# A linear-attention block and a SoLU feed-forward block on one core: a fixed, software-pipelined order on TensorE, with attention five chunks ahead of the input product and that three ahead of the output product

## The chip, the core and the metric

The kernel runs on one core of one Trainium2 chip. The core has five engines, each with its own instruction queue taken in order: TensorE (PE in the profile, with its weight loads listed as PEld), VectorE (DVE), ScalarE (ACT), GpSimd (POOL) and SyncE (SP), which here only starts DMA transfers. Matrix products are written to a small memory called PSUM, and DVE or ACT copy them out. The metric is the device time of one execution in microseconds (us). The profiler lists the clock that was granted to TensorE, as a share of full speed; in this kernel it is 1.0 or 0.5, and shares between these are means.

## The reference

Two blocks follow each other. The first is a recurrence over 768 steps for 4 batches and 8 heads of width 48; the second takes its 3072 x 384 output through two matrix products with a softmax-weighted activation and a normalisation between them.

```python
for t in range(S):
    cur = np.einsum('bhd,bhe->bhde', u[None] * kt, vt)
    y[:, :, t] = np.einsum('bhd,bhde->bhe', rt, state + cur)
    state = w[None, :, :, None] * state + np.einsum('bhd,bhe->bhde', kt, vt)
...
h = x @ w_in                                  # 3072 x 384 times 384 x 1024
sm = softmax(h)
solu = h * sm
ln = (solu - mean(solu)) / np.sqrt(var(solu) + 1e-06) * g_ln
out = ln @ w_out                              # 3072 x 1024 times 1024 x 384
```

## The kernel before

The sequence is cut into 6 chunks of 128 steps. A unit is one batch and one chunk, so there are 24 units; they go chunk by chunk with the four batches side by side, so the state that a unit needs was made four units earlier. A unit is also 128 rows of the feed-forward block.

In a unit, `prepare` (line 590) weighs k with powers of w on POOL (tile `kp`), multiplies r, u and k for the diagonal (`rku`, `own`), writes the diagonal into the score tile `AT`, and turns r and the weighed k on PE (`tr_ps`, `tk_ps`, copied to `rT` by DVE and to `kT` by ACT). `scores` (618) makes the 128 x 128 scores of each head (`at`) and DVE copies their upper triangle into `AT`. `finish` (631) makes the output of attention (`y_ps`, from the state and from `AT` and v), copies it to `x`, and updates the state (`kv_ps`). `ffn_in` (661) turns x (`xt_ps`, copied to `xT`), makes the input product `h_ps`, and lets DVE, ACT and POOL do softmax, product and normalisation, in this order: maximum, exponential, division, `solu`, squares, power, normalised `solu`. `ffn_out` (693) turns `solu` (`t_ps`, copied to `lnT` by halves, the first by DVE and the second by ACT), makes the output product `o_ps`, copies it to `o` and stores it.

The weights come as 64-bit floats, in 14 pieces. `load_weights` fetches a piece as pairs of 32-bit words (`raw`), and `convert` makes 32-bit floats of it with seven operations on DVE and one or two on POOL.

The loop at the end (713 to 736) sets the order in which the code names the work: a load two units ahead, `prepare` one ahead, up to five conversions, `ffn_in` of the unit three back (`LAG`), `scores`, `ffn_out` of the unit three back, `finish`. A scheduler then orders each engine's queue from this, by the code's order and its own estimate of when each operation can start; so on PE the matmuls of different functions may change places. PSUM holds four tiles for everything called `m` (`tr_ps`, `tk_ps`, `y_ps`, `kv_ps`, `xt_ps`, `t_ps`, `o_ps`), two for the scores, and one `h_ps`.

`direct_path` holds all of this; `general_path`, for values of w outside 0.75 to 1.25, stands behind a branch that these inputs do not take.

Of the kernel before, what the change touches and what calls it, by code (L numbers as in the profile page):

```python
# [9 lines left out]
F32 = mybir.dt.float32  # L10
U32 = mybir.dt.uint32
# [385 lines left out]
def direct_path(  # L397
# [56 lines left out]
    def load(i):  # L454
        b, c = units[i]
        for t, src in ((kpads, k), (rpads, r), (vts, v)):
            nc.sync.dma_start(out=t[i % NLD][:, :, 0:D],
                              in_=src[b, :, ts(c, T), :].rearrange("h s d -> s h d"))
# [9 lines left out]
    for q in range(2):  # L468
# [19 lines left out]
    raws = {}  # L488

    def load_weights(j):  # L490
        dst, src, _ = pieces[j]
        raws[j] = wpool.tile([128, dst.shape[1], 2], U32, tag="raw", name="raw", bufs=6)
        nc.scalar.dma_start(out=raws[j].rearrange("p n o -> p (n o)"), in_=src)
# [30 lines left out]

    for j in range(6):
        load_weights(j)
# [14 lines left out]
    for j in range(7):  # L541
        n = 1 << j
# [41 lines left out]
    live = {}  # L584

    def pair(t, a):
        return t[:, 2 * a : 2 * a + 2, :].rearrange("p q d -> p (q d)")


    def prepare(i):  # L590
        b, c = units[i]
        kt, rt = kpads[i % NLD], rpads[i % NLD]
        X = live[i] = {}
        X["kp"] = kp = apool.tile([128, H, P], F32, name="kp")
        nc.gpsimd.tensor_mul(kp.rearrange("p h d -> p (h d)"),  # L595
                             kt.rearrange("p h d -> p (h d)"),
                             kdec.rearrange("p a d -> p (a d)"))
        rku = apool.tile([128, H, D], F32, name="rku")
        nc.gpsimd.tensor_mul(rku, kt[:, :, 0:D], u_bc)  # L599
        nc.gpsimd.tensor_mul(rku, rku, rt[:, :, 0:D])  # L600
        own = small.tile([128, H, 1], F32, name="own")
        nc.vector.tensor_reduce(out=own[:, :, 0], in_=rku, axis=AX.X, op=ALU.add)  # L602
        AT = X["AT"] = apool.tile([128, H, T], F32, name="AT")
        nc.gpsimd.tensor_mul(AT, ident.unsqueeze(1).to_broadcast([128, H, T]),  # L604
                             own.to_broadcast([128, H, T]))
        X["kT"] = apool.tile([128, HP, T], F32, name="kT")
        X["rT"] = apool.tile([128, HP, T], F32, name="rT")
        ps = psM.tile([128, HP, T], F32, tag="m", name="tr_ps")
        for a in range(HP):
            nc.tensor.transpose(ps[:, a, :], pair(rt, a), ident)  # L610
        nc.vector.tensor_mul(X["rT"], ps, fore)
        ps = psM.tile([128, HP, T], F32, tag="m", name="tk_ps")
        for a in range(HP):
            nc.tensor.transpose(ps[:, a, :], pair(kp, a), ident)  # L614
        nc.scalar.copy(out=X["kT"], in_=ps)  # L615
# [15 lines left out]
    def finish(i):  # L631
        b, c = units[i]
        X = live[i]
        vt, AT, St = vts[i % NLD], X["AT"], states[b]
        y_ps = psM.tile([128, H, D], F32, tag="m", name="y_ps")
# [7 lines left out]
        for h in range(H):  # L643
            nc.tensor.matmul(y_ps[:, h, :], AT[:, h, :], vt[:, h, :],  # L644
                             start=first, stop=(h == H - 1), skip_group_check=True)
            first = False
        x = X["x"] = fpool.tile([128, dm], F32, name="x", bufs=LAG + 1)
        nc.scalar.copy(out=x, in_=y_ps.rearrange("p h d -> p (h d)"))
# [11 lines left out]

    def ffn_in(i):
        X = live[i]
        xt_ps = psM.tile([128, KD, 128], F32, tag="m", name="xt_ps")
        for j in range(KD):
            nc.tensor.transpose(xt_ps[:, j, :], X["x"][:, ts(j, 128)], ident)
        xT = fpool.tile([128, KD, 128], F32, name="xT")
        nc.scalar.copy(out=xT, in_=xt_ps)  # L667
        h_ps = psH.tile([128, dff], F32, name="h_ps")
        for n in range(dff // NX):
            for j in range(KD):  # L670
                nc.tensor.matmul(h_ps[:, ts(n, NX)], xT[:, j, :], w_in_sb[:, j, ts(n, NX)],  # L671
                                 start=(j == 0), stop=(j == KD - 1))
# [6 lines left out]
        nc.vector.reciprocal(out=rs, in_=rs)  # L679
        solu = X["solu"] = fpool.tile([128, dff], F32, name="solu")  # L680
        nc.vector.scalar_tensor_tensor(out=solu, in0=h_ps, scalar=rs, in1=e,  # L681
# [10 lines left out]

    def ffn_out(i):
        b, c = units[i]
        X = live.pop(i)
        lnT = fpool.tile([128, KF, 128], F32, name="lnT")
        for g in range(KF // 4):
            t_ps = psM.tile([128, 4, 128], F32, tag="m", name="t_ps")
            for f in range(4):
                nc.tensor.transpose(t_ps[:, f, :], X["solu"][:, ts(4 * g + f, 128)], ident)  # L700
            if g % 2 == 0:
                nc.vector.tensor_copy(out=lnT[:, ts(g, 4), :], in_=t_ps)
            else:
                nc.scalar.copy(out=lnT[:, ts(g, 4), :], in_=t_ps)
        o_ps = psM.tile([128, dm], F32, tag="m", name="o_ps")
        for f in range(KF):
            nc.tensor.matmul(o_ps, lnT[:, f, :], w_out_sb[:, f, :],  # L707
                             start=(f == 0), stop=(f == KF - 1))
        o = fpool.tile([128, dm], F32, name="o")
        nc.scalar.copy(out=o, in_=o_ps)  # L710
        nc.sync.dma_start(out=out[ds(b * S + c * T, T), :], in_=o)

    N = len(units)
    todo = list(range(len(pieces)))
    ahead = 6
    prepare(0)
    for i in range(N + LAG):
        j = i - LAG
        if i + 2 < N:
            load(i + 2)  # L720
        if i + 1 < N:
            prepare(i + 1)
        for _ in range(5):
            if todo:
                convert(todo.pop(0))
                if ahead < len(pieces):
                    load_weights(ahead)
                    ahead += 1
# [51 lines left out]
```

## Time and profile before

| | |
|---|---|
| time, median of 3 runs | 825.41 us (824.98 to 825.49) |
| the profiled execution's own time | 824.45 us |
| its span, first to last instruction | 822.7 us |
| mean granted TensorE clock | 0.768 |
| matmuls on PE | 2220 |
| DMA | 25.83 MB, mean 31 GB/s |

The span is what the profiler's rows cover; the time has some 1.75 us more around it. A busy share is an average over a start (until about 100 us, in which the weights are converted), a steady part, and an end. The rows in the next parts give for each group or instruction its start, its duration, the line of the code, the tiles (output<-inputs) and, in brackets, how long the engine stood idle before it and what released it.

### The profile page before, as it was taken

The numbers are of one execution on the slowest core, as the hardware profiler recorded it, in microseconds if no ns is written. First come the engines' busy times: TensorE is split into PE (matmuls) and PEld (weight loads), VectorE is DVE, ScalarE is ACT, GpSimd is POOL, SyncE is SP. The second block draws the span as 40 slices with busy tenths as digits, with TensorE's granted clock in tenths as the row PEclk, the third lists the DMA queues.
The fourth block names the chain that finished last, engine by engine and source line by source line (L and its number), as shares of the span: only waits on it lengthen the run. The fifth ranks groups of instructions, "written<-read, shape, count | busy, mean of one in ns | idle before, by whom it ended". The sixth has DMA issues, their size and how long they took to land.

```text
span 822.7 us, 5801 instructions
## 1 busy us (share of the span) xinstructions
PE 548.8 (67%) x2220; PEld 351.4 (43%) x2220; DVE 249.9 (30%) x441; ACT 121.2 (15%) x217; POOL 184.3 (22%) x193
## 2 busy tenths in 40 slices
PE   0344575867768568658677686596686696656764
PEld 0244443634535435435345354354353464334332
DVE  6999633122131230231321312212212312221121
ACT  0100011111110110111111101111111212121111
POOL 4655702202212112032022121220220201000000
PEclk9955587778768867877787687777777887789886
DMA  9632101101101011011011010110100000000000
GB/s 237 133 94 63 29 6 33 39 0 39 37 2 39 20 19 39 10 29 39 1 38 27 13 38 11 29 39 0 39 20 0 19 10 10 0 10 10 10 10 14
DMA packets 81990, 25.83 MB, mean 31 GB/s; under 512 B 76961, under 2 KB 80162, under 8 KB 81954
## 3 DMA queue, kind: packets, MB, share of 16 engines
q1 hardware_dynamic: 78336, 18.88, 11.2%
q10 hardware_dynamic: 3618, 6.50, 2.7%
q8 instruction: 19, 0.31, 0.2%
q14 instruction: 17, 0.14, 0.1%
HBM read 20.65 MB, written 4.72 MB: 31 GB/s over the span
## 4 chain that ended last, share of the span: by engine, by line
PE 60%; DVE 18%; POOL 8%; ACT 8%; issue 4%; DMA 1%; ACTq 0%; POOLq 0%
PE h_ps L671 20%; PE o_ps L707 20%; PE y_ps L644 6%; PE t_ps L700 6%; DVE solu L681 4%; POOL AT L604 4%; ACT sq L685 4%; DVE st L675 4%; ACT e L677 4%; POOL kp L595 3%; DVE solu L689 2%; PE tk_ps L614 2%; PE y_ps L639 2%; PE at L625 2%; POOL st L688 2%
## 5 line engine op out<-in xcount | busy, mean ns | idle before, releaser
L671 PE MATMUL h_ps<-w_in_sb,xT 128*128 128x512 f32 x288 | 169.1, 749 | 2.5 <-ACT xT L667 2.5
L707 PE MATMUL o_ps<-w_out_sb,lnT 128*128 128x384 f32 x384 | 165.1, 594 | 0.0
L700 PE MATMUL t_ps<-ident,solu 128*128 128x128 f32 x192 | 46.6, 424 | 164.8 <-DVE solu L689 164.8
L707 PEld LDWEIGHTS o_ps<-w_out_sb,lnT 128*128 128x128 f32 x384 | 88.8, 239 | 69.4 <-issue 30.5
L700 PEld LDWEIGHTS t_ps<-ident,solu 128*128 128x128 f32 x192 | 37.6, 223 | 171.2 <-issue 166.8
L671 PEld LDWEIGHTS h_ps<-w_in_sb,xT 128*128 128x128 f32 x288 | 67.8, 244 | 89.0 <-issue 83.4
L604 POOL TENSOR_TENSOR AT<-ident,own 128x1024 f32<-128x1024 f32 x24 | 45.7, 1903 | 238.9 <-PE y_ps L644 236.6
L675 DVE TENSOR_REDUCE st<-h_ps 128x1 f32<-128x1024 f32 x24 | 29.4, 1225 | 153.0 <-PE h_ps L671 153.0
L644 PE MATMUL y_ps<-vt,AT 128*128 128x48 f32 x384 | 51.3, 289 | 36.1 <-DVE AT L628 24.9
L686 POOL TENSOR_SCALAR st<-st 128x1 f32<-128x1 f32 x24 | 4.6, 192 | 305.6 <-ACT sq L685 305.6
L644 PEld LDWEIGHTS y_ps<-vt,AT 128*128 128x128 f32 x384 | 50.1, 209 | 37.1 <-DVE AT L628 25.4
L655 DVE TENSOR_TENSOR state<-kv_ps,state 128x384 f32<-128x384 f32 x16 | 8.9, 557 | 167.6 <-PE kv_ps L652 167.6
L677 ACT ACTIVATE e<-h_ps,st 128x1024 f32<-128x1024 f32 x24 | 26.7, 1114 | 207.6 <-DVE st L675 207.6
L614 PE MATMUL tk_ps<-ident,kp 128*128 128x128 f32 x96 | 21.4, 363 | 39.8 <-POOL kp L595 39.8
L625 PE MATMUL at<-rT,kT 48*128 48x128 f32 x384 | 42.3, 347 | 5.4 <-ACT kT L615 3.8
L602 DVE TENSOR_REDUCE own<-rku 128x8 f32<-128x384 f32 x24 | 13.2, 549 | 105.7 <-POOL rku L600 105.7
L625 PEld LDWEIGHTS at<-rT,kT 48*128 48x128 f32 x384 | 31.6, 227 | 28.3 <-issue 16.8
L689 DVE TENSOR_SCALAR solu<-solu,st 128x1024 f32<-128x1024 f32 x24 | 19.5, 812 | 54.1 <-POOL st L688 54.1
L599 POOL TENSOR_TENSOR rku<-kpad,u_bc 128x384 f32<-128x384 f32 x24 | 24.4, 1016 | 46.5 <-DMA kpad<-in_k_dram 46.5
L685 ACT ACTIVATE sq<-solu,st 128x1024 f32<-128x1024 f32 x24 | 27.5, 1147 | 48.3 <-DVE st L683 48.3
L710 ACT COPY o<-o_ps 128x384 f32<-128x384 f32 x24 | 11.5, 479 | 149.3 <-PE o_ps L707 149.3
L614 PEld LDWEIGHTS tk_ps<-ident,kp 128*128 128x128 f32 x96 | 14.5, 184 | 44.3 <-POOL kp L595 44.3
(67 smaller groups left out, 515.9 us busy)
## 6 DMA issues: line engine op xcount, KB each, us to landing
kpad<-in_k_dram SPq DMA_DIRECT2D x24, 192.0 KB, 3.2
rpad<-in_r_dram SPq DMA_DIRECT2D x24, 192.0 KB, 3.8
vt<-in_v_dram SPq DMA_DIRECT2D x24, 192.0 KB, 2.7
out_dram<-o SPq DMA_DIRECT2D x24, 192.0 KB, 1.9
raw<-in_moe_w_in_dram ACTq DMA_DIRECT2D x6, 512.0 KB, 6.6
raw<-in_moe_w_out_dram ACTq DMA_DIRECT2D x8, 384.0 KB, 3.1
u_bc<-in_u_dram ACTq DMA_DIRECT2D x1, 192.0 KB, 3.9
wd<-in_w_dram ACTq DMA_DIRECT2D x2, 0.8 KB, 6.1
```

What stands on the lines that cost most here:

```text
L604: nc.gpsimd.tensor_mul(AT, ident.unsqueeze(1).to_broadcast([128, H, T]), own.to_broadcast([128, H, T]))
L614: nc.tensor.transpose(ps[:, a, :], pair(kp, a), ident)
L625: nc.tensor.matmul(pss[q][:, a, :], X["kT"][rows, a, :], X["rT"][rows, a, :], start=True, stop=True)
L644: nc.tensor.matmul(y_ps[:, h, :], AT[:, h, :], vt[:, h, :], start=first, stop=(h == H - 1), skip_group_check=True)
L671: nc.tensor.matmul(h_ps[:, ts(n, NX)], xT[:, j, :], w_in_sb[:, j, ts(n, NX)], start=(j == 0), stop=(j == KD - 1))
L675: nc.vector.tensor_reduce(out=nmax, in_=h_ps, axis=AX.X, op=ALU.max, negate=True)
L677: nc.scalar.activation(out=e, in_=h_ps, func=ACT.Exp, bias=nmax, accum_out=se)
L681: nc.vector.scalar_tensor_tensor(out=solu, in0=h_ps, scalar=rs, in1=e, op0=ALU.mult, op1=ALU.mult, accum_out=tot)
L685: nc.scalar.activation(out=sq, in_=solu, func=ACT.Square, bias=nmu, accum_out=ss)
L689: nc.vector.tensor_scalar(out=solu, in0=solu, scalar1=nmu, scalar2=rstd, op0=ALU.add, op1=ALU.mult)
L700: nc.tensor.transpose(t_ps[:, f, :], X["solu"][:, ts(4 * g + f, 128)], ident)
L707: nc.tensor.matmul(o_ps, lnT[:, f, :], w_out_sb[:, f, :], start=(f == 0), stop=(f == KF - 1))
```

## The change

All 24 units, all tiles and all operations stay. What changes is their order and the number of buffers.

- `prepare` is split into `weigh` (POOL and DVE work) and `turn` (transposes); the transposes of x leave `ffn_in` as `turn_x`, and those of the normalised values leave `ffn_out` as `turn_ln`.
- The loop runs from -2 to N + 8. In iteration i stand: load of i+4, `weigh` of i+3, `turn` of i+2, two conversions, `ffn_in` of i-5, `turn_ln` of i-8, `scores` of i+1, `ffn_out` of i-8, `finish` of i, `turn_x` of i-4.
- The loop stands under a manual schedule for PE: its queue has exactly the order of the code. The queues of the other engines are ordered by the scheduler as before.
- More buffers: v has 6 tiles for 4, `kp` and `AT` 4 for 2, `rT` 3 for 2, `x` 6 for 4, `solu` 5 for 2. `raw` has 5 for 6.

```diff
-    LAG = 3
+    LA, LO = 5, 3
...
-    NLD = 4
+    NLD, NV = 4, 6
...
-    vts = [const.tile([128, H, D], F32, name=f"vt{i}") for i in range(NLD)]
+    vts = [const.tile([128, H, D], F32, name=f"vt{i}") for i in range(NV)]
...
     load(1)
+    load(2)
+    load(3)
...
-    def prepare(i):
+    def weigh(i):
...
-        X["kp"] = kp = apool.tile([128, H, P], F32, name="kp")
+        X["kp"] = kp = apool.tile([128, H, P], F32, name="kp", bufs=4)
...
-        AT = X["AT"] = apool.tile([128, H, T], F32, name="AT")
+        AT = X["AT"] = apool.tile([128, H, T], F32, name="AT", bufs=4)
...
+    def turn(i):
+        X, rt = live[i], rpads[i % NLD]
         X["kT"] = apool.tile([128, HP, T], F32, name="kT")
-        X["rT"] = apool.tile([128, HP, T], F32, name="rT")
+        X["rT"] = apool.tile([128, HP, T], F32, name="rT", bufs=3)
...
-    def ffn_in(i):
+    def turn_x(i):
         X = live[i]
         xt_ps = psM.tile([128, KD, 128], F32, tag="m", name="xt_ps")
...
+    def ffn_in(i):
+        X = live[i]
         h_ps = psH.tile([128, dff], F32, name="h_ps")
...
-        solu = X["solu"] = fpool.tile([128, dff], F32, name="solu")
+        solu = X["solu"] = fpool.tile([128, dff], F32, name="solu", bufs=LO + 2)
...
-    def ffn_out(i):
-        b, c = units[i]
-        X = live.pop(i)
-        lnT = fpool.tile([128, KF, 128], F32, name="lnT")
+    def turn_ln(i):
+        X = live[i]
+        lnT = X["lnT"] = fpool.tile([128, KF, 128], F32, name="lnT")
...
+    def ffn_out(i):
+        b, c = units[i]
+        X = live.pop(i)
         o_ps = psM.tile([128, dm], F32, tag="m", name="o_ps")
...
-    ahead = 6
-    prepare(0)
-    for i in range(N + LAG):
-        j = i - LAG
-        if i + 2 < N:
-            load(i + 2)
-        if i + 1 < N:
-            prepare(i + 1)
-        for _ in range(5):
-            if todo:
-                convert(todo.pop(0))
...
-        if j >= 0:
-            ffn_in(j)
-        if i < N:
-            scores(i)
-        if j >= 0:
-            ffn_out(j)
-        if i < N:
-            finish(i)
+    ahead = 5
+    weigh(0)
+    weigh(1)
+    with tc.manual_schedule(engines={mybir.EngineType.PE}):
+        for i in range(-2, N + LA + LO):
+            j, l = i - LA, i - LA - LO
+            if 0 <= i and i + 4 < N:
+                load(i + 4)
+            if 0 <= i + 3 and i + 3 < N and i + 3 >= 2:
+                weigh(i + 3)
+            if 0 <= i + 2 < N:
+                turn(i + 2)
+            for _ in range(2):
+                if i >= -1 and todo:
+                    convert(todo.pop(0))
...
+            if 0 <= j < N:
+                ffn_in(j)
+            if 0 <= l < N:
+                turn_ln(l)
+            if 0 <= i + 1 < N:
+                scores(i + 1)
+            if 0 <= l < N:
+                ffn_out(l)
+            if 0 <= i < N:
+                finish(i)
+            if 0 <= j + 1 < N:
+                turn_x(j + 1)
```

**PE, one iteration of the steady part.** PE's queue before, from one input product to the next; the number behind a tile's name tells the copies of it apart, and `solu_1715` is what the softmax makes of `h_ps_1702`. The scores' further rows, which repeat `at0` and `at1`, are left out.

```order
L671 MATMUL h_ps_1702<-w_in_sb_105,xT_1700 128x512 x6
L625 MATMUL at0_1835<-rT_1683,kT_1682 128x128
L625 MATMUL at1_1836<-rT_1683,kT_1682 128x128
L700 MATMUL t_ps_1736<-ident_132,solu_1715 128x128 x4
L700 MATMUL t_ps_1742<-ident_132,solu_1715 128x128 x4
L707 MATMUL o_ps_1748<-w_out_sb_106,lnT_1735 128x384 x8
L639 MATMUL y_ps_1760<-state1_186,rT_1571 128x96 x4
L644 MATMUL y_ps_1760<-vt1_91,AT_1568 128x48 x8
L652 MATMUL kv_ps_1775<-vt1_91,kp_1561 128x96 x4
L610 MATMUL tr_ps_1796<-ident_132,rpad3_85 128x128 x4
L614 MATMUL tk_ps_1802<-ident_132,kp_1785 128x128 x4
L665 MATMUL xt_ps_1808<-ident_132,x_1549 128x128 x3
```

The same stretch of PE's queue now. `solu_1142` belongs to the input product three iterations earlier; that of `h_ps_1465` is `solu_1478`.

```order
L678 MATMUL h_ps_1465<-w_in_sb_107,xT_1437 128x512 x6
L706 MATMUL t_ps_1487<-ident_138,solu_1142 128x128 x4
L706 MATMUL t_ps_1493<-ident_138,solu_1142 128x128 x4
L629 MATMUL at0_1499<-rT_1340,kT_1339 128x128
L629 MATMUL at1_1500<-rT_1340,kT_1339 128x128
L717 MATMUL o_ps_1511<-w_out_sb_108,lnT_1486 128x384 x8
L643 MATMUL y_ps_1523<-state0_191,rT_1228 128x96 x4
L648 MATMUL y_ps_1523<-vt0_90,AT_1113 128x48 x8
L656 MATMUL kv_ps_1538<-vt0_90,kp_1106 128x96 x4
L669 MATMUL xt_ps_1545<-ident_138,x_1088 128x128 x3
L614 MATMUL tr_ps_1565<-ident_138,rpad3_85 128x128 x4
L618 MATMUL tk_ps_1571<-ident_138,kp_1442 128x128 x4
```

The turning of the normalised values now reads a tile of an earlier iteration, the scores stand between it and the output product, and the transposes of x stand ahead of those of r and k.

**DVE, one iteration of the steady part.** DVE's queue before, from the maximum over one `h_ps` on:

```order
L675 TENSOR_REDUCE st_1373<-h_ps_1366 128x1
L628 COPY_PREDICATED AT_1344<-later_167,at0_1499 128x4x128
L628 COPY_PREDICATED AT_1344<-later_167,at1_1500 128x4x128
L678 TENSOR_SCALAR st_1373<-st_1373 128x1
L679 RECIPROCAL st_1373<-st_1373 128x1
L681 SCALAR_TENSOR_TENSOR solu_1379,st_1373<-h_ps_1366,st_1373,e_1375 128x1024
L683 TENSOR_SCALAR st_1373<-st_1373 128x1
L689 TENSOR_SCALAR solu_1379<-solu_1379,st_1373 128x1024
L702 COPY lnT_1399<-t_ps_1400 128x512
L655 TENSOR_TENSOR state2_187<-kv_ps_1439,state2_187 128x384
L611 TENSOR_TENSOR rT_1459<-tr_ps_1460,fore_140 128x512
L602 TENSOR_REDUCE own_1902<-rku_1899 128x8
```

And now:

```order
L682 TENSOR_REDUCE st_1360<-h_ps_1353 128x1
L708 COPY lnT_1374<-t_ps_1375 128x512
L632 COPY_PREDICATED AT_1113<-later_173,at0_1387 128x4x128
L685 TENSOR_SCALAR st_1360<-st_1360 128x1
L632 COPY_PREDICATED AT_1113<-later_173,at1_1388 128x4x128
L686 RECIPROCAL st_1360<-st_1360 128x1
L688 SCALAR_TENSOR_TENSOR solu_1366,st_1360<-h_ps_1353,st_1360,e_1362 128x1024
L690 TENSOR_SCALAR st_1360<-st_1360 128x1
L696 TENSOR_SCALAR solu_1366<-solu_1366,st_1360 128x1024
L659 TENSOR_TENSOR state3_194<-kv_ps_1426,state3_194 128x384
L615 TENSOR_TENSOR rT_1452<-tr_ps_1453,fore_146 128x512
L603 TENSOR_REDUCE own_1783<-rku_1780 128x8
```

The copy of the first half of `lnT` has moved from behind the normalisation to right behind the maximum; the rest of the order is nearly the same. In the start of the program, DVE's queue had up to five conversions between the score copies of two units and now has two.

More of the change, by code (lines that the diff above doesn't have):

```diff
@@ L491, in load_weights @@
         dst, src, _ = pieces[j]
[L492 removed]
+        raws[j] = wpool.tile([128, dst.shape[1], 2], U32, tag="raw", name="raw", bufs=5)
         nc.scalar.dma_start(out=raws[j].rearrange("p n o -> p (n o)"), in_=src)
@@ L523, in convert @@
                                     op0=ALU.mult, op1=ALU.mult)
-    for j in range(6):
+    for j in range(5):
         load_weights(j)
@@ L613, in prepare @@
         for a in range(HP):
-            nc.tensor.transpose(ps[:, a, :], pair(kp, a), ident)
+            nc.tensor.transpose(ps[:, a, :], pair(X["kp"], a), ident)
         nc.scalar.copy(out=X["kT"], in_=ps)
@@ L665, in ffn_in @@
             nc.tensor.transpose(xt_ps[:, j, :], X["x"][:, ts(j, 128)], ident)
-        xT = fpool.tile([128, KD, 128], F32, name="xT")
-        nc.scalar.copy(out=xT, in_=xt_ps)
+        X["xT"] = fpool.tile([128, KD, 128], F32, name="xT")
+        nc.scalar.copy(out=X["xT"], in_=xt_ps)
+    def ffn_in(i):
+        X = live[i]
         h_ps = psH.tile([128, dff], F32, name="h_ps")
@@ L670, in ffn_in @@
             for j in range(KD):
-                nc.tensor.matmul(h_ps[:, ts(n, NX)], xT[:, j, :], w_in_sb[:, j, ts(n, NX)],
+                nc.tensor.matmul(h_ps[:, ts(n, NX)], X["xT"][:, j, :], w_in_sb[:, j, ts(n, NX)],
                                  start=(j == 0), stop=(j == KD - 1))
@@ L704, in ffn_out @@
                 nc.scalar.copy(out=lnT[:, ts(g, 4), :], in_=t_ps)
+    def ffn_out(i):
+        b, c = units[i]
+        X = live.pop(i)
         o_ps = psM.tile([128, dm], F32, tag="m", name="o_ps")
         for f in range(KF):
-            nc.tensor.matmul(o_ps, lnT[:, f, :], w_out_sb[:, f, :],
+            nc.tensor.matmul(o_ps, X["lnT"][:, f, :], w_out_sb[:, f, :],
                              start=(f == 0), stop=(f == KF - 1))
```

13 lines of the change are left out of this document (6 added, 7 removed).

## The prediction

> **What bounds the kernel now.** I read the page's head and its chain of waits first, then the waits of TensorE (PE), then one unit of the steady part on PE's timeline, then the granted clock in windows. The page's first two rows say who works and who ends last (busy us by engine; the chain followed back from the end, as shares of the span):
>
> ```profile
> PE 548.8 (67%) x2220; PEld 351.4 (43%) x2220; DVE 249.9 (30%) x441; ACT 121.2 (15%) x217; POOL 184.3 (22%) x193
> PE 60%; DVE 18%; POOL 8%; ACT 8%; issue 4%; DMA 1%; ACTq 0%; POOLq 0%
> ```
>
> PE is busy for 67% and no engine is full; the chain changes from PE to the others and back. PE's rows of one unit (start, duration; a product of the program stands as two matmuls in the trace, a transpose as one, so h_ps counts 12 for 6):
>
> ```profile
> 403.86 1.94 PE L700 MATMUL t_ps<-ident,solu 128*128 128x128 f32 x8 [6.84 <-DVE solu L689]
> 405.73 6.21 PE L707 MATMUL o_ps<-w_out_sb,lnT 128*128 128x384 f32 x16
> 411.77 1.03 PE L639 MATMUL y_ps<-state,rT 128*128 128x96 f32 x8
> 412.64 1.91 PE L644 MATMUL y_ps<-vt,AT 128*128 128x48 f32 x16
> 414.38 1.10 PE L652 MATMUL kv_ps<-vt,kp 128*128 128x96 f32 x8
> 415.32 0.60 PE L610 MATMUL tr_ps<-ident,rpad 128*128 128x128 f32 x4
> 417.80 1.12 PE L614 MATMUL tk_ps<-ident,kp 128*128 128x128 f32 x4 [1.88 <-POOL kp L595]
> ...
> 420.32 7.43 PE L671 MATMUL h_ps<-w_in_sb,xT 128*128 128x512 f32 x12
> 427.68 0.94 PE L625 MATMUL at<-rT,kT 48*128 48x128 f32 x12
> 435.45 1.94 PE L700 MATMUL t_ps<-ident,solu 128*128 128x128 f32 x8 [6.83 <-DVE solu L689]
> ```
>
> A unit takes 435.45 - 403.86 = 31.6 us. PE stands still for 6.83 us of it, while the softmax and normalisation of the unit whose input product it has just made run on DVE, ACT and POOL, and for 1.88 us until POOL has weighed k. Over the kernel the first wait alone is
>
> ```profile
> PE t_ps L700 <- DVE solu L689: 164.8, 24, 7.7
> ```
>
> 164.8 us in 24 units. The waits cost a second time, through the clock. In windows of 3.41 us (length, PE busy with its count, granted clock, then DMA):
>
> ```profile
> 93.32:96.73 3.41, 3.41 (x18) 0.50 0.15 28
> 96.73:100.14 3.41, 3.41 (x19) 0.50 0.75 144
> ...
> 414.17:417.58 3.41, 1.75 (x16) 1.00 0.29 54
> 417.58:420.99 3.41, 3.15 (x12) 0.50 0.63 118
> ...
> 666.75:670.16 3.41, 3.41 (x32) 1.00 0.16 58
> 670.16:673.58 3.42, 3.07 (x16) 1.00 0.00 0
> ...
> 721.36:724.78 3.42, 2.82 (x27) 1.00 0.16 58
> 724.78:728.19 3.41, 3.41 (x8) 1.00 0.00 0
> ```
>
> The clock changes at the edges of such windows. After a window with 1.75 us of work it falls to half (414.17); after 2.82 us of light matmuls (721.36) and after a window full of them (666.75) it stays full; a full window of light matmuls at half clock does not raise it (93.32). So each long wait is followed by matmuls at half speed: the sixteen of o_ps above take 411.77 - 405.73 = 6.04 us, and at full clock, by the rows below, 5.16.
>
> **The change part by part.** The order on PE is now that of the code: input product of unit i-5, turning of the normalised unit i-8, scores of i+1, output product of i-8, end of attention of i. The normalised values that are turned were finished three units ago, so the 6.83 us wait goes; kp is made two units ahead of its turning, so the 1.88 us go. No matmul is added or removed. What PE then needs for a unit, at full clock:
>
> ```profile
> 149.83 2.74 PE L707 MATMUL o_ps<-w_out_sb,lnT 128*128 128x384 f32 x8
> 152.41 1.03 PE L639 MATMUL y_ps<-state,rT 128*128 128x96 f32 x8
> ...
> 669.90 0.60 PE L614 MATMUL tk_ps<-ident,kp 128*128 128x128 f32 x4
> 670.34 0.49 PE L665 MATMUL xt_ps<-ident,x 128*128 128x128 f32 x3
> ...
> 671.60 5.42 PE L671 MATMUL h_ps<-w_in_sb,xT 128*128 128x512 f32 x12
> 676.94 0.94 PE L625 MATMUL at<-rT,kT 48*128 48x128 f32 x12
> ...
> 724.73 5.42 PE L671 MATMUL h_ps<-w_in_sb,xT 128*128 128x512 f32 x12 [0.60 <-ACT xT L667]
> ```
>
> From start to start: h_ps 676.94 - 671.60 = 5.34; o_ps 2 x 2.58 = 5.16; four transposes 0.44, so tr, tk 0.44 each, t_ps (8) 0.88, xt_ps (3) 0.33; scores 16 x 0.94/12 = 1.25; from the first unit's rows, whose clock was full by then, y_ps 0.87 + 1.74 and kv_ps 0.94. Sum 17.4 us against 31.6. 0.1 us for small waits is an estimate: **17.5 us a unit**.
>
> What hides the rest: the output product needs the first half of lnT, and DVE takes h_ps's maximum before it copies that half:
>
> ```profile
> L675 DVE TENSOR_REDUCE st<-h_ps 128x1 f32<-128x1024 f32 x24 | 29.4, 1225 | 153.0 <-PE h_ps L671 153.0
> L702 DVE COPY lnT<-t_ps 128x512 f32<-128x512 f32 x24 | 16.6, 692 | 30.4 <-PE t_ps L700 30.4
> L677 ACT ACTIVATE e<-h_ps,st 128x1024 f32<-128x1024 f32 x24 | 26.7, 1114 | 207.6 <-DVE st L675 207.6
> L681 DVE SCALAR_TENSOR_TENSOR solu<-h_ps,st,e 128x1024 f32<-128x1024 f32 x24 | 30.8, 1284 | 0.8
> ```
>
> 1.23 + 0.69 and two starts of 0.1 give 2.1 us after h_ps; t_ps and scores cover 0.88 + 1.25 = 2.13. It just fits; where scores are missing, at the end, 1.2 us of wait appear. h_ps has one buffer and comes free after maximum, exponential and product, with DVE's copies between them some 5 us (an estimate from these rows), inside the 12 us until the next h_ps. xT's copy waits beside eight transposes (0.88 us against the 0.60 of the last row); without them, at the end, 0.6 us appear. The output of a unit leaves three units later, which costs nothing but the drain. The deeper buffers (kp, AT, solu, vt) only separate users. One raw buffer fewer delays a weight load until the fifth conversion before it is read; at two conversions an iteration that is hidden.
>
> The start changes most in its order. Five conversions stood ahead of each pair of score copies on DVE, now two. In the old start (last steps of four successive conversions at 78.94 and 89.94, the third unit's last copy, the first input product, and DVE's two larger operations of a unit):
>
> ```profile
> 78.94 1.35 DVE L510 SCALAR_TENSOR_TENSOR ex<-raw,ex 128x384 uint32<-128x384 uint32 x1
> ...
> 89.94 0.55 DVE L510 SCALAR_TENSOR_TENSOR ex<-raw,ex 128x384 uint32<-128x384 uint32 x1
> ...
> 91.96 0.72 DVE L628 COPY_PREDICATED AT<-later,at 128x512 f32<-128x512 uint32 x1
> ...
> 99.96 5.49 PE L671 MATMUL h_ps<-w_in_sb,xT 128*128 128x512 f32 x12
> ...
> L628 DVE COPY_PREDICATED AT<-later,at 128x512 f32<-128x512 uint32 x48 | 32.1, 714 | 0.0
> L611 DVE TENSOR_TENSOR rT<-tr_ps,fore 128x512 f32<-128x512 f32 x24 | 16.3, 681 | 21.2 <-PE tr_ps L610 21.2
> ```
>
> A conversion takes 11.0 / 3 = 3.7 us; a unit of attention 2 x 0.71 + 0.68 and two short ones, which I take at 3.2 in all. The old 92.7 held 14 conversions and three units. The first input product now needs ten conversions and five units: 92.7 - 14.7 + 6.4 = 84, and some 9.5 us of PE at half clock behind it (at, y, kv, xt, tr, tk): 94. All 14 conversions and six units are done at 92.7 + 9.6 = 102; the first softmax comes only then, so the second input product starts near 106, the third 11.6 later (5.34 and 6 of attention), the fourth at **129**. From there both products run in each iteration:
>
> - 12 iterations of 17.5 (units 8 to 19 in attention): 210
> - two without kv (16.56): 33
> - two more without tr and tk, with xT's 0.6: 32.6
> - four without attention, 5.34 + 2.1 + 5.16 + 0.33 + 0.6: 54, and a fifth without xt: 12.6
> - three of t_ps and o_ps alone, 0.88 + 0.6 + 5.16: 19.8
>
> That is 362: the last output product ends at 491. Behind it stands what stands now:
>
> ```profile
> 817.35 0.48 ACT L710 COPY o<-o_ps 128x384 f32<-128x384 f32 x1 [6.36 <-PE o_ps L707]
> ```
>
> 822.7 - 817.35 = 5.4. Span 496.5; the profiled execution took 824.45 us with a span of 822.7, so 498; the median, 825.41, lies 1 above it: **499 us**. The start is the loosest term, 129 within 10 either way; a unit may cost 17.0 (weight loads better hidden) or 18.5 (a microsecond of small waits). That is 482 to 525.
>
> [...] Between two products stand y, kv, xt, tr, tk: 4.8 us of light matmuls, eleven instructions of them transposes. The rows that come nearest: the window at 666.75 has y, tr and tk and stays at full clock, and four tk take 0.44 there, against the eight t_ps at half clock in 1.87 us (403.86 to 405.73), 0.94 for four. So transposes run at full clock and do not lower it here. [...]
>
> **The rivals.**
>
> [...] 10%.
>
> *DVE or POOL behind PE.* An engine that takes its queue in order may stand behind a load: POOL's next unit waits for kpad, whose buffer POOL itself frees.
>
> ```profile
> kpad<-in_k_dram SPq DMA_DIRECT2D x24, 192.0 KB, 3.2
> ```
>
> Round that loop go one landing of 3.2 us and at most POOL's whole work of a unit, 184.3/24 = 7.7: 10.9 us, under 17.5. It decides from a landing of 9.8 us; at 12.3 the unit takes 20, +2.5 over 16 units: 540. POOL then also holds back DVE's `own`, which stands ahead of the next maximum. 6%.
>
> *Slower than before: the clock halves in a dense stream.* The quoted stretch at full clock is two windows long, 6.8 us (666.75 to 673.58); whether hundreds of us are granted it no row shows. At half clock throughout a unit takes 2 x 17.4 = 34.8, over the 31.6 of now, and the sum 129 + 2 x 362 = 853, span and all 860. It decides below a granted clock of about 0.55. Against it: the only thing that lowers the clock in these rows is a window with little work in it (414.17). 2%. A milder form, 0.8, gives 129 + 452, near 590: 2%. [...]
>
> *The change doesn't do what it says*: PE's fixed order waits at its head each time, for instance for xT or lnT, and a unit stays above 25 us: 129 + 362 + 8 x 16 = 620. The order shows every producer at least a stage ahead. 3%.
>
> **How the numbers follow.** The forecast has 77%, with its own 482 to 525; the rivals 10, 6, 2, 2, 3. To 482 to 540 belong the first two rivals: range 482 to 540, somewhat over 8 in 10. Faster by over 0.2% (about what a measurement of this kernel can tell from no change): 97%; within 0.2%: 1%; slower: 2%.
>
> **What would show it.** In the new profile: h_ps at 5.4 and o_ps at 5.2 us in every steady unit, clock 1.00 in windows from about 110 us on, t_ps without a wait for solu; a period of 17.5 between t_ps groups; the first h_ps near 94 and the fourth near 129; DVE, ACT and POOL with the same busy time as before. Wrong would be: windows of 0.50 in the steady part, a PE wait of over 1 us for lnT, xT or AT in each unit, or a POOL waiting for kpad beyond DVE's reach.

## The result and the profile after

| | before | after |
|---|---|---|
| time, median | 825.45 us (4 runs, 824.98 to 825.68) | 513.28 us (4 runs, 512.25 to 514.26) |
| ratio, 95% interval | | 0.6218 [0.6205, 0.6232] |
| profiled execution, its span | 824.45, 822.7 us | 512.92, 511.1 us |
| mean granted TensorE clock | 0.768 | 0.938 |

The forecast was 499 us within 482 to 540. The page of the changed kernel: busy time by engine, the chain of waits, and the two products.

```profile
PE 440.5 (86%) x2220; PEld 304.0 (59%) x2220; DVE 263.8 (52%) x441; ACT 119.5 (23%) x217; POOL 189.0 (37%) x193
PE 68%; DVE 22%; DMA 4%; POOL 2%; ACT 1%; issue 1%; ACTq 0%; DVEq 0%; POOLq 0%
L678 PE MATMUL h_ps<-w_in_sb,xT 128*128 128x512 f32 x288 | 129.9, 601 | 10.3 <-DVE solu L688 5.9
L717 PE MATMUL o_ps<-w_out_sb,lnT 128*128 128x384 f32 x384 | 130.3, 492 | 8.0 <-DVE lnT L708 8.0
```

The first row alone splits the gain. The same 2220 matmuls took 548.8 us and take 440.5, which is 108 us, nearly all of it clock (PE's busy time times the missing share of the clock, summed over windows of 3.41 us, is 124 us before and 24 now); PE stood still for 822.7 - 548.8 = 273.9 us and does for 511.1 - 440.5 = 70.6, which is 203 us of waits. Together 311 of span. But the row also speaks against the prediction, which expected DVE's busy time to stay: its 441 operations took 249.9 us and now take 263.8.

PE's timeline of one unit in the steady part:

```profile
271.82 1.04 PE L706 MATMUL t_ps<-ident,solu 128*128 128x128 f32 x8
272.79 1.16 PE L629 MATMUL at<-rT,kT 48*128 48x128 f32 x16
273.90 5.43 PE L717 MATMUL o_ps<-w_out_sb,lnT 128*128 128x384 f32 x16
...
283.91 5.32 PE L678 MATMUL h_ps<-w_in_sb,xT 128*128 128x512 f32 x12
289.06 1.04 PE L706 MATMUL t_ps<-ident,solu 128*128 128x128 f32 x8
```

289.06 - 271.82 = 17.24 us, and no row has a bracket, nor has any of those left out: nothing in the unit waits. Two windows (length, busy time of each engine with its count, granted clock, DMA) show the start and all of the rest:

```profile
60.00:120.00 60.00, 43.82 (x239) 38.34 (x238) 59.99 (x93) 6.91 (x13) 44.13 (x37) 0.70 0.37 83
130.00:480.00 350.00, 338.97 (x1731) 223.75 (x1729) 140.83 (x250) 100.93 (x185) 94.84 (x107) 1.00 0.13 31
```

From 130 us on the clock is 1.00 and PE is busy for 339 of 350 us. Between 60 and 120 us DVE, the third of the busy times, is busy for 59.99 of 60. What PE still waits for beside 20.0 us for a table that both kernels make at the very start (engine and tile, releaser, us, times, longest):

```profile
PE at L629 <- DVE AT L632: 18.1, 5, 5.6
PE tk_ps L618 <- POOL kp L596: 8.7, 1, 8.7
PE o_ps L717 <- DVE lnT L708: 8.0, 11, 1.0
PE h_ps L678 <- DVE solu L688: 5.9, 1, 5.9
PE h_ps L678 <- ACT xT L671: 4.3, 7, 0.6
```

The 164.8 us for solu are gone. Last, the first, second and fourth input product and the last output product, from PE's timeline:

```profile
103.75 5.32 PE L678 MATMUL h_ps<-w_in_sb,xT 128*128 128x512 f32 x12
121.01 6.86 PE L678 MATMUL h_ps<-w_in_sb,xT 128*128 128x512 f32 x12 [5.91 <-DVE solu L688]
...
145.26 5.32 PE L678 MATMUL h_ps<-w_in_sb,xT 128*128 128x512 f32 x12
...
500.21 5.43 PE L717 MATMUL o_ps<-w_out_sb,lnT 128*128 128x384 f32 x16 [0.40 <-DVE lnT L708]
```

From the fourth input product to the end of the last output product are 505.6 - 145.3 = 360 us (362 forecast). The miss of 14 us lies ahead of it: the fourth input product starts at 145.26 for 129, and 2 of these 16 us are made up behind it.

### The profile page after: what moved, and what is told of

Same layout as the page of the kernel before. It is cut to its first block, busy times and chain, and to the rows that moved or that the text cites. A ratio compares the mean times of both kernels' runs of the same rounds, so it can differ in the third digit from the quotient of the medians.

```text
span 511.1 us, 5767 instructions
## 1 busy us (share of the span) xinstructions
PE 440.5 (86%) x2220; PEld 304.0 (59%) x2220; DVE 263.8 (52%) x441; ACT 119.5 (23%) x217; POOL 189.0 (37%) x193
## 4 chain that ended last, share of the span: by engine, by line
PE 68%; DVE 22%; DMA 4%; POOL 2%; ACT 1%; issue 1%; ACTq 0%; DVEq 0%; POOLq 0%
PE o_ps L717 25%; PE h_ps L678 22%; PE y_ps L648 6%; PE at L629 3%; PE y_ps L643 3%; PE kv_ps L656 3%; PE t_ps L706 2%; DVE low L518 2%; DVE st L682 2%; DVE ex L507 2%; DVE ma L515 2%; DVE ma L517 2%; DVE ex L508 2%; DVE ex L510 2%; DVE AT L632 2%; DMA rpad<-in_r_dram 2%
## 5 line engine op out<-in xcount | busy, mean ns | idle before, releaser
L678 PE MATMUL h_ps<-w_in_sb,xT 128*128 128x512 f32 x288 | 129.9, 601 | 10.3 <-DVE solu L688 5.9
L717 PE MATMUL o_ps<-w_out_sb,lnT 128*128 128x384 f32 x384 | 130.3, 492 | 8.0 <-DVE lnT L708 8.0
L717 PEld LDWEIGHTS o_ps<-w_out_sb,lnT 128*128 128x128 f32 x384 | 71.0, 190 | 56.8 <-DVE lnT L708 10.5
L678 PEld LDWEIGHTS h_ps<-w_in_sb,xT 128*128 128x128 f32 x288 | 53.4, 192 | 70.6 <-issue 64.4
L629 PE MATMUL at<-rT,kT 48*128 48x128 f32 x384 | 35.2, 318 | 18.2 <-DVE AT L632 18.1
L710 ACT COPY lnT<-t_ps 128x512 f32<-128x512 f32 x24 | 14.1, 586 | 121.6 <-PE t_ps L706 121.0
L692 ACT ACTIVATE sq<-solu,st 128x1024 f32<-128x1024 f32 x24 | 27.5, 1148 | 51.7 <-DVE st L690 51.7
L596 POOL TENSOR_TENSOR kp<-kpad,kdec 128x512 f32<-128x512 f32 x24 | 34.2, 1428 | 12.4 <-PE kv_ps L656 12.4
L632 DVE COPY_PREDICATED AT<-later,at 128x512 f32<-128x512 uint32 x48 | 33.5, 724 | 1.8
L652 ACT COPY x<-y_ps 128x384 f32<-128x384 f32 x24 | 11.5, 479 | 90.4 <-PE y_ps L648 90.4
L688 DVE SCALAR_TENSOR_TENSOR solu<-h_ps,st,e 128x1024 f32<-128x1024 f32 x24 | 30.8, 1284 | 0.8
L684 ACT ACTIVATE e<-h_ps,st 128x1024 f32<-128x1024 f32 x24 | 26.9, 1119 | 15.4 <-DVE st L682 15.4
L706 PEld LDWEIGHTS t_ps<-ident,solu 128*128 128x128 f32 x192 | 22.5, 141 | 12.0 <-issue 10.2
```

The lines of the kernel that those rows point to most:

```text
L596: nc.gpsimd.tensor_mul(kp.rearrange("p h d -> p (h d)"), kt.rearrange("p h d -> p (h d)"), kdec.rearrange("p a d -> p (a d)"))
L629: nc.tensor.matmul(pss[q][:, a, :], X["kT"][rows, a, :], X["rT"][rows, a, :], start=True, stop=True)
L632: nc.vector.copy_predicated(A4[:, :, q, :], later.to_broadcast([128, HP, T]), pss[q])
L678: nc.tensor.matmul(h_ps[:, ts(n, NX)], X["xT"][:, j, :], w_in_sb[:, j, ts(n, NX)], start=(j == 0), stop=(j == KD - 1))
L684: nc.scalar.activation(out=e, in_=h_ps, func=ACT.Exp, bias=nmax, accum_out=se)
L692: nc.scalar.activation(out=sq, in_=solu, func=ACT.Square, bias=nmu, accum_out=ss)
```

## The experiments

Two things were open. What carries the gain: the distances between the stages, the fixed order on PE, or the buffers; and is a wait really paid twice? And why is the start 16 us late: is DVE simply full there, or is something slowing its operations? All kernels are edits of the changed one, save the fifth; the 441 operations of DVE and the 2220 matmuls stay unless said otherwise. Experiments 1 to 5 were timed once each, 6 to 11 four times.

**1. The output product back in the iteration of its input product.**

```diff
-    LA, LO = 5, 3
+    LA, LO = 5, 0
```

> The output product in the iteration of its input product (LO 0), all else as in the changed kernel: attention still five units ahead, PE's order still fixed. Theory (the three units between the two products carry the gain): t_ps waits again for solu, 6 to 8 us in each unit, the windows behind the wait fall to 0.50, and the period is 17.2 + 7 + 4 to 5.5 of half clock = 28 to 30 us; with the start as in the changed kernel the time is 660 to 720 us. Rival (a fixed order with attention five ahead would have been enough): a period below 19, a time below 560.

761.12 us. PE's timeline of one unit, then the trace cut at the 3.41 us edges of the clock (window, PE, PEld, DVE, ACT, POOL, clock):

```profile
338.40 5.32 PE L678 MATMUL h_ps<-w_in_sb,xT 128*128 128x512 f32 x12
351.41 1.94 PE L706 MATMUL t_ps<-ident,solu 128*128 128x128 f32 x8 [7.70 <-DVE solu L696]
353.28 2.08 PE L629 MATMUL at<-rT,kT 48*128 48x128 f32 x16
355.29 6.77 PE L717 MATMUL o_ps<-w_out_sb,lnT 128*128 128x384 f32 x16
...
366.65 5.32 PE L678 MATMUL h_ps<-w_in_sb,xT 128*128 128x512 f32 x12
```

```profile
344.28:347.70 3.42, 0.00 (x0) 0.00 (x0) 2.02 (x4) 1.21 (x2) 0.00 (x0) 1.00 0.00 0
347.70:351.11 3.41, 0.00 (x0) 0.00 (x0) 1.10 (x4) 1.24 (x2) 0.74 (x2) 0.51 0.00 0
351.11:354.52 3.41, 3.11 (x20) 2.81 (x21) 0.85 (x2) 0.58 (x1) 0.00 (x0) 0.50 0.02 5
354.52:357.94 3.42, 3.42 (x12) 2.06 (x11) 1.33 (x2) 0.00 (x0) 0.00 (x0) 0.50 0.00 0
357.94:361.35 3.41, 3.41 (x12) 2.01 (x11) 0.00 (x0) 0.00 (x0) 0.00 (x0) 0.99 0.00 0
```

The unit takes 366.65 - 338.40 = 28.25 us, as the theory said: 17.24, 7.70 of wait, and the rest, 3.3, is half clock. The window without work is followed by three at half clock, one of them idle too. The rival falls: a fixed order with attention five ahead is not enough. The time lies above the expected 660 to 720 all the same. The first input product stands at 104.1, the last at 736.2, so the period holds from the first unit on, (736.2 - 104.1) / 23 = 27.5 us each; with 104 us of start and the 23 us behind the last input product, 660 to 720 us have room for only 19 to 20 periods of 28 to 30.

**2. The same, with the wait filled by transposes.** Sixty transposes of the identity stand ahead of t_ps:

```diff
+    def fill(n):
+        ps = psM.tile([128, HP, T], F32, tag="m", name="fill_ps")
+        for a in range(n):
+            nc.tensor.transpose(ps[:, a % HP, :], ident, ident)
...
             if 0 <= l < N:
+                fill(60)
                 turn_ln(l)
```

> As the kernel before it with LO 0, but 60 transposes of the identity, whose results nothing reads, stand on PE ahead of t_ps in each iteration: 60 x 0.11 = 6.6 us at full clock, so PE works through the wait and hardly stands still. Nothing of the computation is left out. Theory (the long wait costs twice, and transposes count as work): the clock stays 1.00 in the steady windows, the products keep 5.3 and 5.2 us, the period is 17.2 + 6.6 + 0.5 to 2 = 24 to 26 us, the time 570 to 630 us, less than with LO 0 alone although PE does more. Rival (a stretch of transposes is no work for the clock): 0.50 behind the fillers, which themselves take up to 14 us there, a period of 31 or more, a time above 740 us. [...]

696.85 us, 64 less than without the filling, with 1440 matmuls more:

```profile
339.14 5.32 PE L678 MATMUL h_ps<-w_in_sb,xT 128*128 128x512 f32 x12
344.29 6.71 PE L727 MATMUL fill_ps<-ident 128*128 128x128 f32 x60
352.16 1.06 PE L706 MATMUL t_ps<-ident,solu 128*128 128x128 f32 x8 [1.16 <-DVE solu L696]
353.15 1.16 PE L629 MATMUL at<-rT,kT 48*128 48x128 f32 x16
354.25 5.43 PE L717 MATMUL o_ps<-w_out_sb,lnT 128*128 128x384 f32 x16
...
364.26 5.32 PE L678 MATMUL h_ps<-w_in_sb,xT 128*128 128x512 f32 x12
```

The wait for the softmax is as long as before, but PE works through it, the clock of the execution is 0.982 for 0.794, and what follows runs at full speed: scores 1.16 for 2.08, output product 5.43 for 6.77. So the clock's part of a wait is a cost of its own. The period is 364.26 - 339.14 = 25.1 us, as expected; the whole is above the expected 570 to 630 us as in 1, since the period holds from the first unit on ((674.6 - 103.0) / 23 = 24.9 us). The transposes take 6.71 / 60 = 0.11 us each at full clock and keep it: 1.00 from 344.3 to 351.1 us, where they run, and 1.00 from 352.1 to 359.5 us behind them. The rival, 0.50 behind the fillers, falls.

**3. The scheduler's order on PE**, everything else as changed:

```diff
-    with tc.manual_schedule(engines={mybir.EngineType.PE}):
+    if True:
```

> The changed kernel without the manual schedule: the scheduler orders PE's queue, from the same code with the same distances and buffers. Theory (the distances between the stages carry the gain, the fixed order only keeps them): producers are units ahead whatever the order, clock about 1.00, period 17.2 to 19, time 505 to 540 us. Rival (without the fixed order the scheduler puts matmuls whose inputs come late at the head of PE's queue, and the waits return): period 20 or more, time above 570 us.

505.18 us, at the lower edge of the expected 505 to 540. The theory holds, and more: without the fixed order the kernel is faster. It was timed again below (9).

**4. `weigh` left out from unit 4 on**, that is, POOL's work and the `own` of DVE (20 operations). These units take the `kp` and `AT` tiles of units 0 to 3, so what the kernel puts out is not the block's result; only its times are of use.

```diff
+    kept = {}
...
     def weigh(i):
         kt, rt = kpads[i % NLD], rpads[i % NLD]
         X = live[i] = {}
+        if i >= 4:
+            X["kp"], X["AT"] = kept[i % 4]
+            return
...
+        kept[i] = kp, AT
```

> From unit 4 on POOL and DVE leave out weigh (kp, rku, own and the diagonal of AT are not made anew); these units use the kp and AT tiles of units 0 to 3. Theory (the conversions were slower than forecast because POOL's work of weigh runs beside them): the conversions take near 3.7 us again after the first units, those of 0.35 us no longer take 1.2 to 2, the first h_ps comes 7 to 12 us sooner (103.75 in the changed kernel), the fourth 10 to 16 us sooner (145.26), DVE's busy time falls from 263.8 to about 237 (14 of contention, 24 x 0.5 of own), time 496 to 504 us. Rival (DVE is simply full there, or the loads of the weights set the pace): the first h_ps at 101 or later, time 507 to 513 us. The steady period stays 17.2 in both, since PE sets it.

486.98 us, below the expected 496 to 504. The first input product stands at 82.06 (103.75 in the changed kernel), the fourth at 120.03 (145.26), DVE is busy for 226.0 us (237 expected). The theory holds and had the size too small: 22 and 25 us for 7 to 12 and 10 to 16. Not all of it need be the slowing of DVE: the `own` operations are gone too, and PE waits less for AT (8.3 us for 18.1); 7 parts the two. How it comes about is seen in the changed kernel, in DVE's timeline of two conversions and POOL's beside it:

```profile
81.94 2.04 DVE L510 TENSOR_SCALAR ex<-ex 128x384 uint32<-128x384 uint32 x1
83.91 1.16 DVE L508 TENSOR_SCALAR ex<-ex 128x384 uint32<-128x384 uint32 x1
84.99 1.35 DVE L512 SCALAR_TENSOR_TENSOR ex<-raw,ex 128x384 uint32<-128x384 uint32 x1
86.26 1.42 DVE L510 TENSOR_SCALAR ex<-ex 128x384 uint32<-128x384 uint32 x1
```

```profile
81.78 1.99 POOL L605 TENSOR_TENSOR AT<-ident,own 128x1024 f32<-128x1024 f32 x1
83.73 1.11 POOL L600 TENSOR_TENSOR rku<-kpad,u_bc 128x384 f32<-128x384 f32 x1
84.92 1.00 POOL L601 TENSOR_TENSOR rku<-rku,rpad 128x384 f32<-128x384 f32 x1
85.88 1.58 POOL L596 TENSOR_TENSOR kp<-kpad,kdec 128x512 f32<-128x512 f32 x1
```

Each DVE operation ends 0.2 to 0.4 us behind the end of the POOL operation that was running when it came to its turn (83.98 and 83.77, 85.07 and 84.84, 86.34 and 85.92, 87.68 and 87.46): four operations take 5.7 us. The same four in DVE's timeline of the kernel without that work:

```profile
69.61 0.35 DVE L510 TENSOR_SCALAR ex<-ex 128x384 uint32<-128x384 uint32 x1
69.88 0.35 DVE L508 TENSOR_SCALAR ex<-ex 128x384 uint32<-128x384 uint32 x1
70.15 0.55 DVE L512 SCALAR_TENSOR_TENSOR ex<-raw,ex 128x384 uint32<-128x384 uint32 x1
70.62 0.35 DVE L510 TENSOR_SCALAR ex<-ex 128x384 uint32<-128x384 uint32 x1
```

They take 70.97 - 69.61 = 1.4 us. Ends tied to those of POOL, 0.2 to 0.4 us behind them four times in a row, speak for waiting for the end of an instruction, not for a slower rate. What the two engines share there no row shows.

**5. The kernel before, with the output product one unit later and nothing else.**

```diff
-        if j >= 0:
-            ffn_out(j)
+        if j >= 1:
+            ffn_out(j - 1)
...
```

(`solu` gets a third buffer, and the loop one more iteration.)

> The kernel before with one edit: the output product one unit later than the input product (solu with 3 buffers for 2), everything else as before: prepare in one piece, attention three ahead, two buffers of kp and AT, the scheduler's order. Theory (one unit between the two products is what carries the gain in the steady part): no wait for solu, clock mostly 1.00, a wait of up to 2 us for kp or AT stays; period 17.3 to 20 us, the first h_ps near 100 as before; 100 + 24 x 17.3 to 20 + 10 to 15 of end: time 525 to 595 us. Rival (the split of prepare, the deeper kp and AT or the distance of attention is needed too): t_ps or at waits for POOL's work, the clock falls again, a period above 23, a time above 660 us.

560.6 us: 265 of the 312 us come from this one edit. Two of PE's waits now:

```profile
PE tk_ps L614 <- POOL kp L595: 31.7, 17, 8.8
...
PE t_ps L700 <- DVE solu L689: 2.2, 1, 2.2
```

The wait for solu has gone, but for one of 2.2 us, and the one for kp has stayed (39.8 us in the kernel before); the mean period is (536.8 - 99.6) / 23 = 19.0 us, by the first and the last input product.

**6, 7, 8. The start: attention two ahead; less work on POOL; both.** In 6, `LA` is 2 instead of 5. These are units of one batch and one chunk: what the title calls five chunks ahead is five units, a little over one chunk of the sequence. In 7 the diagonal of AT and the factor g of the output weights go from POOL to ACT:

```diff
-        nc.gpsimd.tensor_mul(AT, ident.unsqueeze(1).to_broadcast([128, H, T]),
-                             own.to_broadcast([128, H, T]))
+        for h in range(H):
+            nc.scalar.activation(out=AT[:, h, :], in_=ident, func=ACT.Copy, scale=own[:, h])
...
-            nc.gpsimd.tensor_scalar(out=dst, in0=low, scalar1=g_sb[:, f : f + 1], scalar2=1.0,
-                                    op0=ALU.mult, op1=ALU.mult)
+            nc.scalar.activation(out=dst, in_=low, func=ACT.Copy, scale=g_sb[:, f : f + 1])
```

> The changed kernel with attention two chunks ahead of the input product instead of five (LA 2, LO 3); PE's order fixed as before. Theory (after the start PE is full, so the time is the start's idle time of PE plus its work; input products that begin three iterations earlier fill that idle time): the same steady period of 17.2, the first h_ps at 66 to 80 for 103.75, time 494 to 506 us. Rival (DVE is full until all conversions are done, and the softmax that is pulled into that stretch, 4.1 us of DVE a unit, delays the conversions by as much): time 508 to 516 us.

> The changed kernel with two works moved from POOL to ACT, which is idle for nine tenths of the start: the diagonal of AT (eight ACT operations of 128x128 for one of POOL of 128x1024, 1.94 us) and the factor g of the output weights (0.74 us of POOL a piece). Theory (what POOL does beside the conversions makes DVE's conversions slow): with the two gone, 5 x 1.94 + 7 x 0.74 = 15 of POOL's 46 us between 55 and 116 us, the first h_ps comes 6 to 11 us sooner, DVE's busy time falls from 263.8 to 250 to 257, time 501 to 507 us. Rival (only DVE's own work counts, or what the leaving out of weigh saved was a wait for POOL's results): DVE's busy time above 260, time 510 to 516 us.

> Both of the two edits before it: attention two ahead (LA 2), and the diagonal of AT and the factor g on ACT. Theory (the start's idle time of PE is what is left, and each takes a part of it): between 484 and 498 us, less than either alone. Rival (the two remove the same idle time): within 2 us of the better of the two.

| | time, median of 4 | ratio to the kernel before, 95% |
|---|---|---|
| 6, attention two units ahead | 498.52 us | 0.6042 [0.6031, 0.6053] |
| 7, diagonal and g on ACT | 502.82 us | 0.6078 [0.6052, 0.6104] |
| 8, both | 493.58 us | 0.5974 [0.5946, 0.6002] |

All three times lie where the theories put them. In 6 the first four input products start at 63.16 (66 to 80 was expected), 84.13, 101.68 and 117.81, each of the last three behind a wait for solu (10.05, 2.25, 3.14 us), and the last conversion ends at 125.9 instead of 116.1: the rival's mechanism, softmax that delays conversions, is there too, but takes back only a part. In 7 the first input product stands at 94.44, and the page's first row says

```profile
PE 435.0 (87%) x2220; PEld 298.0 (59%) x2220; DVE 244.5 (49%) x441; ACT 177.9 (35%) x417; POOL 133.0 (26%) x161
```

DVE's 441 operations, none of which was touched, take 19 us less than in the changed kernel, 244.5 us where 250 to 257 were expected. That tells the slowing from the other reading of experiment 4, that only a wait for POOL's results was saved: the profile lists a wait for a result apart from the busy time (153.0 us ahead of the maximum in the kernel before). The two edits together gain 19.7 us, less than 14.8 and 10.5 added: they fill partly the same idle time.

**9, 10, 11. The scheduler's order again, with 7, and with 6 and 7.**

> The changed kernel without the manual schedule once more, timed beside the kernel before: one execution gave 505.18 us, 8 below the fixed order. If the fixed order costs the start some 8 us (it holds ready matmuls of attention and transposes behind ones that wait for DVE), the median is 503 to 507 us; if that was one execution's chance, 510 to 515.

> Attention five ahead, the diagonal of AT and the factor g on ACT, and PE's order left to the scheduler. If the scheduler's order and the relief of POOL remove different idle time of PE in the start: 493 to 499 us (502.8 with the fixed order). If both fill the same waits for AT: 500 to 504.

> Attention two ahead, the two works on ACT, PE's order left to the scheduler: the three edits that helped alone (498.5, 502.8 and 505.2 us). If each leaves idle time of PE in the start that the others remove: 483 to 491 us; if the start is down to DVE's own work by now, as the 493.6 us of the first two together suggest, 491 to 496.

| | time, median of 4 | ratio to the kernel before, 95% |
|---|---|---|
| 9, order left to the scheduler | 502.67 us | 0.6083 [0.6068, 0.6099] |
| 10, that with 7 | 495.02 us | 0.5985 [0.5963, 0.6007] |
| 11, that with 6 and 7 | 478.98 us | 0.5804 [0.5792, 0.5816] |

The fixed order costs 10.6 us; 502.67 lies just below the 503 to 507 of the expectation, which looked for that cost in the start. In the trace of 9 the idle time ahead of the two products is what has shrunk, 10.3 to 1.2 and 8.0 to 3.3:

```profile
L717 PE MATMUL o_ps<-w_out_sb,lnT 128*128 128x384 f32 x384 | 131.5, 496 | 3.3 <-DVE lnT L708 3.3
L678 PE MATMUL h_ps<-w_in_sb,xT 128*128 128x512 f32 x288 | 131.1, 605 | 1.2 <-ACT xT L671 0.9
```

The idle time ahead of both was 18.3 us and is 4.5; that is more than the gain, since the matmuls themselves take somewhat longer (PE is busy for 444.8 us, 440.5 with the fixed order). Nearly all of the gain is in the drain, the end in which attention and scores have run out. The 18th input product starts at 384.79 us, and at 385.41 with the fixed order: 0.6 of the 8.5 us between the two spans (502.6 and 511.1). Behind it the scheduler starts to turn the normalised values ahead of the input product:

```profile
414.25 0.71 PE L706 MATMUL t_ps<-ident,solu 128*128 128x128 f32 x5
415.01 5.42 PE L678 MATMUL h_ps<-w_in_sb,xT 128*128 128x512 f32 x12
420.27 0.49 PE L706 MATMUL t_ps<-ident,solu 128*128 128x128 f32 x3
420.60 5.33 PE L717 MATMUL o_ps<-w_out_sb,lnT 128*128 128x384 f32 x16
```

DVE then copies the first half of lnT while the input product runs, at 414.88 here, ahead of the maximum at 420.47, and o_ps waits for nothing. With the fixed order the copy stands behind the maximum (424.64 behind 423.50) and o_ps waits 1.04 us for it. A unit without attention takes 13.71 us with the fixed order and 12.01 in 9.

The tenth lies where the gains of 7 and 9 nearly add up. The eleventh, with the whole computation, is 34 us faster than the changed kernel and below both of its expectations: PE is busy for 91% of its span, the last conversion ends at 112.5, and by then four input products have begun. The reading that DVE's own work alone sets the start by then falls; which of the scheduler's moves lets the three edits gain nearly the sum of 14.8, 10.5 and 10.6 us, where the first two alone overlap, was not tried. Against the eighth, 10 of the 14.7 us between the two spans (491.9 and 477.2) are there by the fifth input product, at 122.92 for 133.17, so here the scheduler's order pays in the start too.

## Why the prediction was right, and where it was off

- **Waits and clock: right.** No wait for solu behind the start, clock 1.00 from 130 us on, 5.15 us from the start of h_ps to what follows and 5.26 for o_ps (5.34 and 5.16 in the sum), 17.24 us a unit for 17.5. The prediction has kp made two units ahead of its turning; the loop makes it one ahead (`weigh` of i+3, `turn` of i+2), and that was enough. The two terms that were added for each unit, the softmax wait and its half clock, are shown apart by 1 and 2: filling the wait with transposes leaves it as long as it is and still saves 64 us.
- **The lnT copy and xT: right in size.** Where scores are missing PE waits 1.04 us for lnT (1.2 forecast), without the eight transposes 0.62 us for xT (0.6); eleven and seven times, 12.3 us in all. From the fourth input product to the end 360 us for 362, and that is no luck of the sum: its six terms, 210, 33, 32.6, 54, 12.6 and 19.8, measure 207.6, 32.5, 32.6, 54.8, 12.8 and 20.0. The tail, from the last copy of o on, is 511.1 - 505.7 = 5.4 as forecast.
- **The start: the term that was mis-sized.** Two prices of a conversion were wrong. For the four conversions that the first input product no longer needs the prediction took 3.7 us each, "11.0 / 3". Over all fourteen, the busy times of DVE's conversion rows sum to 66.8 us in the kernel before, 4.8 each: the three that were read were cheap ones, with almost no weighing on POOL beside them. That error is not the delay, since with 4.8 the first input product would have been forecast still earlier. The delay is the other: 102 for the end of all conversions is the old 92.7 with three units added, so it holds the old price of the conversions, and that price is not the conversions' own. In the changed kernel they sum to 82.4 us, 5.9 each; with two of POOL's works on ACT (7) to 68.3, and without `weigh` from unit 4 on to 56.6, 4.0 each. The row of one operation shows it, before, after and without `weigh`, grouped by shape:

```profile
L506 DVE TENSOR_SCALAR ex<-ex 128x384 uint32<-128x384 uint32 x8 | 3.6, 451 | 0.0
```

```profile
L508 DVE TENSOR_SCALAR ex<-ex 128x384 uint32<-128x384 uint32 x8 | 6.9, 863 | 0.0
```

```profile
L508 DVE TENSOR_SCALAR ex<-ex 128x384 uint32<-128x384 uint32 x8 | 3.7, 466 | 0.0
```

  Between 40 and 93 us of the old kernel POOL weighed two units; between 55 and 116 us of the new one it weighs five. 82.4 - 66.8 = 15.6 us more of conversions is about the delay that is found: the last conversion ends at 116.1 for 102, the second input product starts at 121.0 for 106, the fourth at 145.3 for 129. Three signs that the prediction itself had named failed: the first h_ps near 94 (103.75), the fourth near 129, and DVE with the same busy time as before (263.8 for 249.9); the last points at the cause. That the time still lies within the range owes something to luck: 129 was given 10 us either way and is 16 off, and the room for it was meant for a unit of 18.5 us and for rivals that did not come.
- **Rivals.** The first of the five, half a clock in each light stretch (10%), which the range counts in: no run shows it; the clock was 1.00 from 130 to 480 us, though between two products stand 4.75 us of light matmuls. POOL behind a load: no wait of PE for POOL in the steady part. A dense stream that halves the clock, or holds it at 0.8: 350 us at 1.00, and no run shows the 0.8. A fixed order that waits at its head: not in the steady part. In the drain it did: the prediction had these waits in its sum, 1.2 and 0.6 us, but took them as given, and with the scheduler's order most of them go; most of its 10.6 us (9) lie there.
- **What carried the gain.** Not the fixed order (9) and not the five units between attention and input product (6), which both cost time; one unit between the two products gives 265 of the 312 us (5). Of the remaining 47 a part is the wait for kp, 31.7 us there and 8.7 here, and another that for AT, 31.3 us there (26.9 and 4.4) and 18.1 here; how this divides between the split of `prepare` and the deeper buffers was not tried.

## What to carry to other kernels

A dependent chain on the other engines between two products was hidden here by one unit of distance between them (265 of the 312 us, 5); distance beyond need cost at both ends (15 us for three units of attention here, of which 4.8 are shorter waits for lnT and xT in the drain, 7.5 us for 12.3). An order that is right for the steady part need not be right for the drain, where the work that covered a copy has run out (up to 1.04 us a unit for lnT here). Where the clock falls after an idle window, as in 1, a wait's price is its length and the half speed behind it (7.70 and 3.3 us in a unit), so that work that fills it can pay: sixty transposes a unit saved 64 us (2). When work is moved beside other work, read the durations again for the new neighbours: a price of DVE's conversions held here only for what POOL did at that time (4.8 us each before, 5.9 in the changed kernel, 4.0 without `weigh` from unit 4 on).

## What was not expected of the hardware

- DVE operations that took 0.35 us without `weigh` beside them (69.61 in 4) took 1.16 to 2.04 us in the changed kernel, where a POOL operation was running (81.94); they ended 0.2 to 0.4 us after it. What `weigh` does on POOL from unit 4 on is worth 27 us of DVE time (263.8 - 226.0, less 20 `own` of 0.54 us).
- In 1, after a window of 3.41 us without work (344.28), three windows at half clock followed, the last of them full of work (354.52 above, 3.42 us busy at 0.50), before the clock came back (0.99 at 357.94); the unit lost 3.3 us more than its gap of 7.70.
- Sixty transposes in a row, 6.71 us without any other work on PE, kept the full clock (1.00 from 344.3 to 351.1 us in 2).
